# Half of wq of two heads, loaded onto partitions 0 to 63 by transfers that run on four DMA engines

## The chip, the cores and the metric

The kernel runs on one NeuronCore of a Trainium2 chip. The core has five instruction streams that run side by side and wait for one another by semaphores: TensorE (PE; its weight loads are listed as PEld), VectorE (DVE), ScalarE (ACT), GpSimd (POOL) and SyncE (SP), which here issues nearly all the transfers. Sixteen DMA engines move the data from HBM, the chip's main memory, into SBUF, the on-chip memory of 128 partitions; TensorE writes its products into PSUM. The metric is the device time of one launch in microseconds (us), lower is better.

## The reference

Two layers, each an attention block with a cached K and V and then a mixer block, are applied to two rows of 512 numbers:

```python
B, Sq, D = 2, 1, 512
Hq, Hkv, Sk, Dh = 32, 8, 32768, 128
x = x + _A_ref(_layernorm(x), A_k_cache, A_v_cache, A_wq, A_wo)   # attention
x = x + _B_ref(_layernorm(x), B_w1, B_b1, B_w2, B_b2)             # mixer
x = x + _A_ref(_layernorm(x), A_k_cache, A_v_cache, A_wq, A_wo)
x = x + _B_ref(_layernorm(x), B_w1, B_b1, B_w2, B_b2)
# _A_ref: q = x @ wq; scores = q k^T * Dh**-0.5; p = softmax(scores); o = p v; return o @ wo
# _B_ref: u = gelu(h * w1 + b1) over F = 1792; y = u @ w2 + b2
```

Each of the 2 x 8 pairs of a batch row and a KV head has 32768 keys and 32768 values of 128 float32 numbers, 16.8 MB of each. Both layers read the same caches and the same weights. The caches of all pairs do not fit in SBUF, so the second layer reads most of them again: the profile counts 1063 MB read from HBM. All arithmetic is float32.

## The kernel before

**Units.** The work of one (layer, batch row, head) is a unit. It has a K phase and a V phase of 64 column groups each, a group being 128 partitions x 512 numbers. A step is four groups of one phase. `Order` writes out the sequence of steps: the K phase of a unit alternates with the V phase of the unit before it. In K steps `k_step` (L360) multiplies four query rows with the keys into a PSUM tile `scores`; softmax parts run on VectorE and ScalarE; in V steps `v_step` (L428) multiplies the exponentials with the values into `acc`. At a unit's end `out_1` and `out_2` (L471, L492) multiply with wo into the PSUM tile `rows`. At the two places where a batch row passes from layer 0 to layer 1 the mixer runs between V steps, and the query of the next layer waits for it.

**Memory.** All keys, values and weights land in one SBUF tile `mem` of 106 cells, a cell being one group (2 KB per partition). A cell is free again when its last reader has run.

**Order of the loads.** `plan_loads` walks a list of what will be asked for, in the order of the steps, and gives each load a place in `mem` and a step behind which it may be issued; its own cost numbers choose between places. All loads are issued by SP, in that order, through one queue (q1 in the profile; the function `load`, L899 for weights, L904 for K and V). SP issues in program order: a load whose cells are not free yet holds up all the loads behind it. The usual load of keys or values is half a phase, 32 cells, 8 MB, and two to three such loads are under way or queued at a time, so that a load lands some 50 us after its issue.

**Weights.** wq and wo of a head are 128 partitions x 2048 numbers each, 1 MB, four cells. wq of the head is asked for 16 steps ahead of the first K step that uses it and is free again at that step. For heads 6 and 7 the weights stay for both layers; for the others they are loaded once in each layer. `wide_products` (L325) multiplies the layernormed input `xw` (four pieces of 128 partitions x 32 columns, one for each quarter `d` of the 512 inputs) with the quarter `d` of wq. The result is the raw query of the head in PSUM tile `bcast`, with one quarter's partial sum in each group of 32 partitions; `narrow_products` (L332) adds the quarters and puts them into `qz`, from which `k_step` reads.

**What other traffic there is.** ACT issues three small transfers on a queue of its own, q10: the input columns, the small weights `cols`, and one row of 512 results (2 KB, one partition) from `row` to `out_dram`. The last result leaves on SP's queue as four rows of 128. The page of the profile also lists two queues of kind "instruction", q8 and q14. They carry the program itself: q8 moved 1.23 MB, which for the 19128 matmuls and weight loads of the page is 64 bytes each.

Of the kernel before, what the change touches and what calls it, by code (L numbers as in the profile page):

```python
# [8 lines left out]
F32 = mybir.dt.float32  # L9
# [4 lines left out]
P = 128  # L14
# [24 lines left out]
STEP_US = 1.6  # L39
ASK_Q = 16  # L40
ASK_O = 8


class Order:
# [75 lines left out]
def plan_loads(order, weights, busy):  # L120
# [24 lines left out]
    while i < len(asked) or weights:  # L145
        if weights and (i == len(asked) or weights[0][0] <= asked[i][0]):
            _, name, last = weights.pop(0)
            label, sizes, stays = ("W", name, 0), (WCELLS,), True
        else:
            _, kind, u, g = asked[i]  # L150
            label, stays = (kind, u, g), (kind, u, g) in order.kept
            n = 1
            while (
                i + n < len(asked)
                and asked[i + n][1:] == (kind, u, g + n)
                and (g + n) % HALF
                and ((kind, u, g + n) in order.kept) == stays
            ):
# [44 lines left out]


@with_exitstack
def gqa_mixer_kernel(ctx: ExitStack, tc: tile.TileContext, x, kt, v, wqo, cols, out):
    nc = tc.nc
    B, D = out.shape
    HKV = wqo.shape[0]
# [43 lines left out]
    misc = pfix.tile([P, G], F32, name="misc")  # L253
    S = [const.tile([P, G], F32, name=f"S{k}") for k in range(2)]
    xw = const.tile([P, DT, 32], F32, name="xw")
    RAW = B
    xT = {}
    turn = [0, 0, 0]
# [23 lines left out]
    def first_input():  # L282
# [16 lines left out]
        for b in range(B):  # L299
            xT[b] = xcols[:, b, :]  # L300
            nc.vector.tensor_scalar_mul(xw[:, :, b], cen[:, b, :], rs[:, b : b + 1])

    def row_tile():
        return work.tile([P, D], F32, name="row", bufs=1)

# [15 lines left out]
    def wide_products(us, wq):  # L321

        q_ps[us] = pfix.tile([P, G], F32, name="bcast")
        for d in range(DT):
            nc.tensor.matmul(q_ps[us][32 * d : 32 * d + 32, :], xw[:, d, :], wq[:, d, :], start=True, stop=True)  # L325

    def narrow_products(us, side):

# [487 lines left out]
    for u in order.units:  # L816
# [60 lines left out]
        at(e + 3, unread, u, G)  # L877
        at(e + 4, change_3, y, us=1.0)
        at(e + 4, unread, u, G // 2)
        assert e + 4 < first["K", y]  # L880

    for x, _, y in order.changes:
# [10 lines left out]
    def load(label, n, a):  # L893
        kind, u, g = label
        if kind == "W":
            part, layer, h = u
            w = D * R
            at_w = 0 if part == "q" else w
            nc.sync.dma_start(cells(a, n), wqo[h][:, at_w : at_w + w])  # L899
            (wq_sb if part == "q" else wo_sb)[layer, h] = cells(a, n).rearrange("p (t c) -> p t c", t=DT)  # L900
            return
        layer, b, h = u
        src = (kt if kind == "K" else v)[b * HKV + h, g // HALF, :, (g % HALF) * G : (g % HALF + n) * G]
        nc.sync.dma_start(cells(a, n), src)  # L904
# [10 lines left out]
        load(label, n, a)  # L915
    constants()
    first_input()
    for step in range(3):
        make_q(opening_q, step)
    for p, (kind, u, g) in enumerate(steps):  # L920
# [8 lines left out]
def _layout(A_x, A_k_cache, A_v_cache, A_wq, A_wo, B_w1, B_b1, B_w2, B_b2):  # L929
# [9 lines left out]
    none = np.zeros_like(w2)  # L939
    w2z = np.stack([none, w2], axis=2).reshape(P, -1)  # L940
    cols = [w1, b1, w2z, none[:, :1], np.broadcast_to(B_b2.reshape(1, 1), (P, 1))]
    return {
        "x": np.ascontiguousarray(A_x.reshape(B * (D // P), P).T),
        "kt": np.ascontiguousarray(kt).reshape(U, 2, DH, HALF * G),
        "v": A_v_cache.reshape(U, 2, P, HALF * G),
        "wqo": np.concatenate([wq.reshape(HKV, P, -1), wo.reshape(HKV, DH, -1)], axis=2),
        "cols": np.concatenate(cols, axis=1),
    }


_INS = ["x", "kt", "v", "wqo", "cols"]


# [20 lines left out]
```

## Time and profile before

| what | value |
|---|---|
| time, median of 3 runs | 2498.51 us (2497.92 to 2499.63) |
| time of the profiled execution | 2500.69 us |
| its span, first to last instruction | 2498.9 us |
| read from HBM | 1063.29 MB, 426 GB/s over the span |
| busy: TensorE matmul / VectorE / ScalarE | 54% / 8% / 8% |
| DMA engines, mean busy share in each of the first 39 of 40 slices | 9 tenths or more |
| granted TensorE clock, mean | 0.765 |

The profiled execution is 2.2 us longer than the median of the runs. In the page, the digits of part 2 are tenths of busy time in 40 equal slices; part 4 follows the work that ended last back to its start; part 5 groups instructions by line. In an answer on DMA for a short stretch of time, "packets" counts the records that start in that stretch, "under 512 B" those of them that are smaller than 512 bytes. Among them is one record of 4 bytes for each DMA engine that has finished its part of a transfer: the engine's count on the semaphore of that transfer. A transfer on sixteen engines has sixteen such marks. The records do not say which engine they stand on.

### The profile page before, as it was taken

The numbers are of one execution on the slowest core, as the hardware profiler recorded it, in microseconds if no ns is written. First come the engines' busy times: TensorE is split into PE (matmuls) and PEld (weight loads), VectorE is DVE, ScalarE is ACT, GpSimd is POOL, SyncE is SP. The second block draws the span as 40 slices with busy tenths as digits, with TensorE's granted clock in tenths as the row PEclk, the third lists the DMA queues.
The fourth block names the chain that finished last, engine by engine and source line by source line (L and its number), as shares of the span: only waits on it lengthen the run. The fifth ranks groups of instructions, "written<-read, shape, count | busy, mean of one in ns | idle before, by whom it ended". The sixth has DMA issues, their size and how long they took to land.

```text
span 2498.9 us, 21072 instructions
## 1 busy us (share of the span) xinstructions
PE 1343.6 (54%) x9564; PEld 376.6 (15%) x9564; DVE 211.3 (8%) x600; ACT 187.4 (8%) x582; POOL 5.2 (0%) x18
## 2 busy tenths in 40 slices
PE   3445455545445544556775774555444544464567
PEld 1111111111111111111121221111111111111113
DVE  1000000000000000001110110000000000000012
ACT  0100000000000000001110210000000000000021
POOL 0000000000000000000000000000000000000000
PEclk8777777777777767778887886777777777777788
DMA  9999999999999999999999999999999999999996
GB/s 419 435 435 431 430 435 432 433 427 436 434 431 435 433 431 428 430 432 411 408 429 422 410 429 435 432 430 436 432 434 431 434 436 430 434 427 435 433 432 280
DMA packets 34946, 1064.64 MB, mean 426 GB/s; under 512 B 4133, under 2 KB 4137, under 8 KB 5034
## 3 DMA queue, kind: packets, MB, share of 16 engines
q1 hardware_dynamic: 34568, 1063.27, 99.1%
q8 instruction: 75, 1.23, 0.2%
q14 instruction: 13, 0.11, 0.0%
q10 hardware_dynamic: 290, 0.04, 0.0%
HBM read 1063.29 MB, written 0.00 MB: 426 GB/s over the span
## 4 chain that ended last, share of the span: by engine, by line
DMA 63%; PE 24%; another core or an unknown queue 11%; DVE 1%; issue 0%; ACT 0%; SPq 0%; POOLq 0%; POOL 0%; DVEq 0%; ACTq 0%
DMA mem<-in_v_dram 35%; DMA mem<-in_kt_dram 28%; PE acc L428 13%; PE scores L360 8%; PE misc L332 1%; PE rows L492 0%; PE bcast L325 0%; PE misc L384 0%; PE misc L451 0%; PE misc L657 0%; SPq L904 0%; ACT S L410 0%; PE misc L378 0%; PE misc L471 0%
## 5 line engine op out<-in xcount | busy, mean ns | idle before, releaser
L428 PE MATMUL acc<-mem,S 128*16 128x512 f32 x4080 | 598.9, 719 | 589.9 <-DMA mem<-in_v_dram 581.6
L360 PE MATMUL scores<-mem,qz 128*32 128x512 f32 x4096 | 598.6, 726 | 532.1 <-DMA mem<-in_kt_dram 532.1
L410 ACT ACTIVATE S<-S,neg 128x128 f32<-128x128 f32 x256 | 129.6, 509 | 2213.0 <-DVE S L405 1188.9
L360 PEld LDWEIGHTS scores<-mem,qz 128*32 128x32 f32 x4096 | 142.8, 127 | 915.0 <-issue 819.5
L428 PEld LDWEIGHTS acc<-mem,S 128*16 128x16 f32 x4080 | 127.5, 107 | 904.5 <-issue 818.8
L370 DVE TENSOR_REDUCE mx<-scores 128x1 f32<-128x512 f32 x64 | 44.3, 692 | 797.5 <-PE scores L360 789.7
L405 DVE STREAM_TRANSPOSE S<-scores 128x512 f32<-128x512 f32 x64 | 45.5, 711 | 125.1 <-PE acc L428 125.1
L410 ACT ACTIVATION_READ_ACCUMULATOR S<-S,neg 128x1 f32 x256 | 47.8, 187 | 0.0
L492 PE MATMUL rows<-mem,oz 128*2 128x512 f32 x248 | 44.1, 794 | 0.3 <-DVE oz L481 0.3
L380 DVE TENSOR_REDUCE m<-misc 1x4 f32<-1x128 f32 x32 | 8.9, 279 | 381.4 <-PE misc L378 381.4
L453 DVE RECIPROCAL rl<-misc 128x4 f32<-128x4 f32 x32 | 5.8, 183 | 382.1 <-PE misc L451 382.1
L462 DVE SCALAR_TENSOR_TENSOR row<-acc,quad,row 128x128 f32<-128x128 f32 x96 | 33.7, 351 | 3.4
L460 DVE TENSOR_SCALAR row<-acc,quad 128x128 f32<-128x128 f32 x32 | 11.2, 351 | 172.7 <-PE acc L428 172.7
L481 DVE TENSOR_TENSOR oz<-misc,rl 128x4 f32<-128x4 f32 x32 | 5.2, 162 | 222.8 <-PE misc L471 222.3
L471 PEld LDWEIGHTS misc<-head,row 128*128 128x128 f32 x64 | 14.0, 274 | 52.2 <-issue 38.3
L325 PE MATMUL bcast<-mem,xw 128*32 128x512 f32 x144 | 20.7, 636 | 1.7 <-POOL x_rs L298 1.7
L451 PEld LDWEIGHTS misc<-both,one 128*128 128x128 f32 x64 | 13.8, 271 | 49.7 <-issue 46.8
L471 PE MATMUL misc<-head,row 128*128 128x4 f32 x64 | 16.8, 334 | 7.3 <-DVE row L462 7.3
L332 PEld LDWEIGHTS misc<-selg,row 128*128 128x128 f32 x128 | 17.3, 210 | 19.6 <-issue 10.2
L576 ACT ACTIVATE row<-bcast,bias,scale 128x512 f32<-128x512 f32 x21 | 16.3, 778 | 38.1 <-PE rows L560 16.1
L332 PE MATMUL misc<-selg,row 128*128 128x2 f32 (+1 forms) x128 | 18.7, 268 | 0.8 <-DVE row L317 0.8
L378 PE MATMUL misc<-ident,mxa 128*1 128x128 f32 x64 | 17.0, 360 | 2.0 <-DVE mxa L376 2.0
(137 smaller groups left out, 282.1 us busy)
## 6 DMA issues: line engine op xcount, KB each, us to landing
mem<-in_v_dram SPq DMA_DIRECT2D x13, 4096.0 KB, 25.1
mem<-in_v_dram SPq DMA_DIRECT2D x37, 1024.0 KB, 9.5
mem<-in_kt_dram SPq DMA_DIRECT2D x15, 2048.0 KB, 18.1
mem<-in_kt_dram SPq DMA_DIRECT2D x30, 1024.0 KB, 9.9
mem<-in_wqo_dram SPq DMA_DIRECT2D x28, 1024.0 KB, 38.5
mem<-in_kt_dram SPq DMA_DIRECT2D x6, 4096.0 KB, 29.4
mem<-in_kt_dram SPq DMA_DIRECT2D x2, 6144.0 KB, 25.1
mem<-in_v_dram SPq DMA_DIRECT2D x3, 2048.0 KB, 38.3
```

Of the source, the lines that this page charges most:

```text
L325: nc.tensor.matmul(q_ps[us][32 * d : 32 * d + 32, :], xw[:, d, :], wq[:, d, :], start=True, stop=True)
L332: nc.tensor.matmul(pt[:, r * n : (r + 1) * n], q_row[us][:, r * DH : (r + 1) * DH], side, start=True, stop=True,)
L360: nc.tensor.matmul(sc_ps[u, half][32 * row : 32 * row + 32, :], qz[:, at : at + 32], cells(at_cell["K", u, g], 1), start=(i == 0), stop=(i ...
L370: nc.vector.tensor_reduce(mx[u][:, half : half + 1], sc_ps[u, half], axis=AX.X, op=ALU.max)
L378: nc.tensor.matmul(pm[:1, :P], mxa, ident, start=True, stop=True)
L405: nc.vector.transpose(S[half], sc_ps[u, half])
L410: nc.scalar.activation(s[:, :, h], s[:, :, h], AF.Exp, bias=neg[u][:, h : h + 1], scale=SCALE, accum_out=lsum[u][:, half, h : h + 1],)
L428: nc.tensor.matmul(acc[32 * row : 32 * row + R * QT, :], S[half][:, col : col + R * QT], vc, start=(g < NG), stop=(g >= quads - NG),)
L462: nc.vector.scalar_tensor_tensor(asb[u], acc[:, t * DH : (t + 1) * DH], quad[:, t : t + 1], asb[u], op0=ALU.mult, op1=ALU.add)
L471: nc.tensor.matmul(po_of[u][:, :R], asb[u], head, start=True, stop=(u != order.last))
L492: nc.tensor.matmul(rows[32 * r : 32 * r + B, :], oT[u][:, 2 * r + 1 - b : 2 * r + 3 - b], wo_of(u)[:, r, :], start=False, stop=(u == order ...
L576: nc.scalar.activation(hid[key, f], px[key], AF.Gelu_apprx_tanh, bias=shift[key][:, f : f + 1], scale=slope[key][:, f : f + 1],)
```

## The change

Two loads of wq are changed, `LOWER`: that of head 5 in layer 0 and that of head 1 in layer 1. The 26 other weight loads stay as they are. Of these two, the first half (quarters d = 0 and 1; 128 partitions x 1024 numbers, 512 KB) is loaded as before. The second half (quarters 2 and 3, also 512 KB) comes by two transfers of 256 KB from a new input array `low`. Each goes to 32 partitions x 2048 numbers: the first to partitions 0 to 31, the second to 32 to 63, in four cells of their own, so that the whole weight now takes six cells in place of four. On the side of HBM each of these transfers reads four groups of 8 rows, and a ninth row of zeros between the groups keeps them from being one run: the outermost size of the source is 4. A partition p of these 64 holds, for each of the two quarters, the 512 numbers of input row p and behind them those of input row 64 + p. `low` holds all eight heads, of which two are read.

`wide_products` then needs two matmuls of 64 rows in place of one of 128 for the quarters 2 and 3. The upper 64 partitions of `xw` for these quarters are copied onto partitions 0 to 63 of a new tile `high` by `lift`, once at the start and once behind each passage to layer 1. The scratch space for dynamic DMA is halved (256 to 128).

```diff
+LOWER = (("q", 0, 5), ("q", 1, 1))
+LOWER_CELLS = 6
...
-            label, sizes, stays = ("W", name, 0), (WCELLS,), True
+            label, sizes, stays = ("W", name, 0), (LOWER_CELLS if name in LOWER else WCELLS,), True
...
+    high = const.tile([P // 2, DT // 2, 32], F32, name="high")
...
+    def lift():
+
+        nc.vector.tensor_copy(high, xw[P // 2 :, DT // 2 :, :])
...
         for d in range(DT):
-            nc.tensor.matmul(q_ps[us][32 * d : 32 * d + 32, :], xw[:, d, :], wq[:, d, :], start=True, stop=True)
+            to = q_ps[us][32 * d : 32 * d + 32, :]
+            if d < DT // 2 or wq.shape[1] == DT:
+                nc.tensor.matmul(to, xw[:, d, :], wq[:, d, :], start=True, stop=True)
+                continue
+            half, k = P // 2, d - DT // 2
+            nc.tensor.matmul(to, xw[:half, d, :], wq[:half, DT // 2 + 2 * k, :], start=True, stop=False)
+            nc.tensor.matmul(to, high[:, k, :], wq[:half, DT // 2 + 2 * k + 1, :], start=False, stop=True)
...
+        at(e + 7, lift)
...
+            if u in LOWER:
+                nc.sync.dma_start(cells(a, DT // 2), wqo[h][:, : w // 2])
+                for k in range(2):
+                    to = cells(a + DT // 2, DT)[32 * k : 32 * k + 32, :]
+                    nc.sync.dma_start(to, low[h, k][:, :8, :])
+                wq_sb[layer, h] = cells(a, n).rearrange("p (t c) -> p t c", t=n)
+                return
...
+    low = np.zeros((HKV, 2, 4, 9, 4 * G), np.float32)
+    part = wq[:, :, D // P // 2 :, :].reshape(HKV, 2, 2, 4, 8, -1, G).transpose(0, 2, 3, 4, 5, 1, 6)
+    low[:, :, :, :8, :] = part.reshape(HKV, 2, 4, 8, 4 * G)
...
-    nc = bacc.Bacc("TRN2", target_bir_lowering=False, num_devices=1, dynamic_dma_scratch_size=256)
+    nc = bacc.Bacc("TRN2", target_bir_lowering=False, num_devices=1, dynamic_dma_scratch_size=128)
```

On SP, around the load of wq for head 5 in layer 0, the issues and their waits were these (the last number is partitions x numbers; `mem_74` is the SBUF tile `mem`, `in_wqo_dram` the weights; the names behind "waits" are semaphores, those of DMA lanes and that of TensorE, `PE_49`):

```order
L904 DMA mem_74<-in_kt_dram 128x16384 [waits DMAHW3_49,PE_49]
L899 DMA mem_74<-in_wqo_dram 128x2048 [waits DMAHW7_49]
L904 DMA mem_74<-in_v_dram 128x16384 [waits DMAHW4_49,PE_49]
L899 DMA mem_74<-in_wqo_dram 128x2048 [waits PE_49]
L904 DMA mem_74<-in_v_dram 128x16384 [waits DMAHW5_49,PE_49]
```

and are now these, with the new array as `in_low_dram`:

```order
L925 DMA mem_74<-in_kt_dram 128x16384 [waits DMAHW3_49,PE_49]
L914 DMA mem_74<-in_wqo_dram 128x1024 [waits DMAHW7_49]
L917 DMA mem_74<-in_low_dram 32x1x2048 [waits PE_49]
L917 DMA mem_74<-in_low_dram 32x1x2048
L925 DMA mem_74<-in_v_dram 128x16384 [waits DMAHW4_49]
L920 DMA mem_74<-in_wqo_dram 128x2048 [waits PE_49]
L925 DMA mem_74<-in_v_dram 128x16384 [waits DMAHW5_49,PE_49]
```

One issue became three, and the wait for TensorE that held the wo load now stands at the first of the two `in_low_dram` issues, ahead of the V load, which has to wait behind it. The loads ahead and behind keep their sequence, their sizes and, but for the wo load that follows (cells 6 to 9 in place of 4 to 7), their cells. The planner puts the changed load 11 steps later, behind step 274 in place of 263 (850 in place of 839 for the second one), since the two more cells were last read by wo of the unit before, and with it the V load behind it 3 steps later. At the second load, that of head 1 in layer 1, the same rows change in the same way.

On TensorE, in the V steps of the unit that runs when the changed wq has come, before:

```order
L428 MATMUL acc<-mem,S_91 16x512 x12
L325 MATMUL bcast<-mem,xw 32x512 x4
L428 MATMUL acc<-mem,S_91 16x512 x4
L428 MATMUL acc<-mem,S_92 16x512 x8
L451 MATMUL misc<-both,one 128x4
```

and now:

```order
L441 MATMUL acc<-mem,S_91 16x512 x12
L334 MATMUL bcast<-mem,xw 32x512 x2
L337 MATMUL bcast<-mem,xw 32x512
L338 MATMUL bcast<-mem,high 32x512
L337 MATMUL bcast<-mem,xw 32x512
L338 MATMUL bcast<-mem,high 32x512
L441 MATMUL acc<-mem,S_91 16x512 x4
L441 MATMUL acc<-mem,S_92 16x512 x8
L464 MATMUL misc<-both,one 128x4
```

Four matmuls became six, in the same place among the V matmuls.

More of the change, by code (lines that the diff above doesn't have):

```diff
@@ L205, in gqa_mixer_kernel @@
 @with_exitstack
-def gqa_mixer_kernel(ctx: ExitStack, tc: tile.TileContext, x, kt, v, wqo, cols, out):
+def gqa_mixer_kernel(ctx: ExitStack, tc: tile.TileContext, x, kt, v, wqo, low, cols, out):
     nc = tc.nc
@@ L917, in gqa_mixer_kernel @@
     first_input()
+    lift()
     for step in range(3):
@@ L946, in _layout @@
         "wqo": np.concatenate([wq.reshape(HKV, P, -1), wo.reshape(HKV, DH, -1)], axis=2),
+        "low": low,
         "cols": np.concatenate(cols, axis=1),
     }
-_INS = ["x", "kt", "v", "wqo", "cols"]
+_INS = ["x", "kt", "v", "wqo", "low", "cols"]
 def kernel(A_x, A_k_cache, A_v_cache, A_wq, A_wo, B_x, B_w1, B_b1, B_w2, B_b2):
```

## The prediction

> **What bounds the kernel now.** I read the page first.
>
> ```profile
> span 2498.9 us, 21072 instructions
> ...
> DMA  9999999999999999999999999999999999999996
> GB/s 419 435 435 431 430 435 432 433 427 436 434 431 435 433 431 428 430 432 411 408 429 422 410 429 435 432 430 436 432 434 431 434 436 430 434 427 435 433 432 280
> DMA packets 34946, 1064.64 MB, mean 426 GB/s; under 512 B 4133, under 2 KB 4137, under 8 KB 5034
> ...
> q8 instruction: 75, 1.23, 0.2%
> ...
> q10 hardware_dynamic: 290, 0.04, 0.0%
> ...
> DMA 63%; PE 24%; another core or an unknown queue 11%; DVE 1%; issue 0%; ACT 0%; SPq 0%; POOLq 0%; POOL 0%; DVEq 0%; ACTq 0%
> ```
>
> The DMA engines are busy in every slice but the last, at up to 436 GB/s, which is 27.2 GB/s for each of the sixteen. The chain that ended last is mostly transfers. The stages say the same: from 100 to 2470 us the DMA share is 1.00 or 1.01 (at 417 GB/s in the stage in the middle, where layer 0 passes to layer 1), and TensorE is busy half the time.
>
> ```profile
> core 0: us, PE busy (x) PEld busy (x) DVE busy (x) ACT busy (x) POOL busy (x), PEclk, DMA share, GB/s
> 100.00:1100.00 1000.00, 502.94 (x3510) 135.50 (x3510) 70.73 (x199) 52.84 (x200) 0.00 (x0) 0.74 1.00 432
> 1180.00:1450.00 270.00, 190.71 (x1368) 54.53 (x1372) 36.13 (x108) 44.36 (x104) 2.17 (x4) 0.83 1.01 417
> 1450.00:2470.00 1020.00, 541.82 (x3795) 150.46 (x3788) 79.23 (x219) 69.37 (x228) 0.54 (x1) 0.76 1.00 432
> ```
>
> So bytes bound the kernel, and the change moves no byte more or less. What it changes is which engines carry them. That matters only if the engines are not equally late, so I looked at the end marks (records of 4 bytes) of single 8 MB loads: early in the run; just ahead of the first changed load (five stretches: 702.0 to 702.45, to 703.8, 703.8 to 705.2, 705.2 to 707.7); just ahead of the second (2055.0 to 2055.7, to 2056.9, 2058.2 to 2060.4); near the end (2416.25 to 2416.535, to 2418.5, 2418.5 to 2420.9, 2420.9 to 2423).
>
> ```profile
> DMA packets 37, 1.38 MB, mean 510 GB/s; under 512 B 16, under 2 KB 16, under 8 KB 16
> ...
> DMA packets 9, 0.33 MB, mean 728 GB/s; under 512 B 4, under 2 KB 4, under 8 KB 4
> DMA packets 22, 0.92 MB, mean 510 GB/s; under 512 B 8, under 2 KB 8, under 8 KB 8
> DMA packets 7, 0.46 MB, mean 328 GB/s; under 512 B 0, under 2 KB 0, under 8 KB 0
> DMA packets 27, 1.25 MB, mean 498 GB/s; under 512 B 8, under 2 KB 8, under 8 KB 8
> ...
> DMA packets 10, 0.39 MB, mean 563 GB/s; under 512 B 4, under 2 KB 4, under 8 KB 4
> DMA packets 23, 0.98 MB, mean 517 GB/s; under 512 B 8, under 2 KB 8, under 8 KB 8
> DMA packets 19, 0.72 MB, mean 328 GB/s; under 512 B 8, under 2 KB 8, under 8 KB 8
> ...
> DMA packets 13, 0.40 MB, mean 1387 GB/s; under 512 B 6, under 2 KB 6, under 8 KB 7
> q10 hardware_dynamic: 2, 0.00, 2.0%
> DMA packets 25, 0.99 MB, mean 438 GB/s; under 512 B 9, under 2 KB 9, under 8 KB 10
> DMA packets 16, 1.05 MB, mean 437 GB/s; under 512 B 0, under 2 KB 0, under 8 KB 0
> DMA packets 23, 0.98 MB, mean 468 GB/s; under 512 B 8, under 2 KB 8, under 8 KB 8
> ```
>
> At 62.9 to 65.6 us all sixteen engines end a load within 2.7 us. At 702 eight end within 1.8 us, then none for 1.4 us, then the other eight; from the fourth to the last it is 707.7 - 702.45 = up to 5.2 us. At 2055 it is 2060.4 - 2055.7 = 4.7 us, at 2416 up to 6.4 us. Eight engines fall behind. All sixteen get the same bytes of data, so something else takes their time, and the only other traffic of any size is the program itself:
>
> ```profile
> q8 instruction: 19, 0.31, 0.2%
> ```
>
> This is the queue's row for 0 to 705 us: 19 fetches, over eight engines 2.4 each, for a lag of 3 to 5 us, so an estimated 1.5 us of an engine per fetch. A consumer waits for all sixteen marks. The lagging eight are the ones that set the end, and a byte taken from them should be time.
>
> **The change, part by part.** *The bytes.* An engine carries 1 MB / 16 = 64 KB of a weight. Now it carries 32 KB in the first half, and four engines carry 256 KB / 4 = 64 KB of each of two transfers on top: 160 KB for these four, 32 KB for the other twelve. At 27.2 GB/s the twelve save 1.2 us and the four lose 3.6 us. If the four are among the leading ones, they need a lead of 3.6 + 1.2 = 4.8 us over the last. They have 5.2 at the first load. They have 4.7 at the second, and the gap grows from there to 6.4. Then the load ends 1.2 us earlier on the engines that set its end: -1.2 us twice, **-2.4 us**.
>
> Do the four lead? The page's 4133 records under 512 B are 289 of q10's 290 and 3844 others, which is 240 x 16 + 4. SP issues 241 loads and stores, all of 128 rows but the last, of four rows: a transfer whose outermost size is four does run on four engines. [...] The row of q10 above is the store of one row of 512 results, one data record and one mark. It had to stand between two records of some engine, and its mark falls with the first five marks of the big load: the engine that takes a one-row transfer is one of the five earliest. [...]
>
> *The later issue.* SP now holds three loads back until wo of the unit before is used.
>
> ```profile
> 679.89 0.41 SPq L899 DMA_DIRECT2D mem<-in_wqo_dram  x1
> 699.12 0.33 SPq L904 DMA_DIRECT2D mem<-in_v_dram  x1
> 713.07 0.33 SPq L899 DMA_DIRECT2D mem<-in_wqo_dram  x1
> 718.22 0.33 SPq L904 DMA_DIRECT2D mem<-in_v_dram  x1
> ...
> 711.97 1.03 PE L492 MATMUL rows<-mem,oz 128*2 128x512 f32 x8
> 727.65 9.22 PE L360 MATMUL scores<-mem,qz 128*32 128x512 f32 x64 [9.50 <-DMA mem<-in_kt_dram]
> 749.49 3.39 PE L428 MATMUL acc<-mem,S 128*16 128x512 f32 x16 [12.61 <-DMA mem<-in_v_dram]
> 757.61 1.04 PE L325 MATMUL bcast<-mem,xw 128*32 128x512 f32 x8
> ```
>
> The first half still goes at about 680. The two others and the V load of 699 go at 713, when L492 has run, and then wo: four issues of some 0.4 us, until 715. The K load ahead lands at 727.6, and even the leading engines, 6 us ahead, have work until 721. No engine runs dry, so the 33 and 14 us of delay cost nothing; the cover is 6 us. The weight still lands in its turn, by 732, and is read at 757.6. What is queued behind the held issues on SP is only the load of 718. The second place has the same spacing.
>
> *TensorE* does two more matmuls per changed load (L325 took 1.04 us for four, so +0.5 us) in V steps ahead of which it stood idle for 12.61 us: nothing. *VectorE* copies 64 x 64 numbers three times:
>
> ```profile
> 15.24 0.23 DVE L346 COPY qz<-misc 128x4 f32<-128x4 f32 x2 [1.96 <-PE misc L332]
> 26.03 8.47 PE L360 MATMUL scores<-mem,qz 128*32 128x512 f32 x64 [10.82 <-DMA mem<-in_kt_dram]
> ```
>
> Small copies take 0.15 us there, and the opening has 10.82 us of cover ahead of the first keys. The scratch space is not on any path here.
>
> *The sum*: against the profiled execution, 2500.69 - 2.4 = 2498.3 us; the median of the runs stands 2.18 lower, 2498.51 - 2.4 = **2496.1 us**. This is 0.1%, half of the 0.2% that a measurement of this kernel can about tell from no change.
>
> **The rivals.** *The four are not all leaders (slower).* If one of them is among the lagging eight, it gets +3.6 us each time, and the end with it: +7.2, 2505.7 us. It decides from a single lagging engine on. [...]
>
> *The two narrow loads share a way into SBUF with other engines.* [...] 128 KB take 4.8 us alone and 9.6 us at half rate: the four would be 8.4 us later relative to their old place, against a lag of the others of 5.2 to 6.4 us that has grown by 1 us or so until a stage's end. That is +1 to +2 us instead of -1.2 each time, together about +3: 2501.6 us. I take nothing for the sum, as the rate per engine in all rows is that of one engine alone. [...]
>
> *It doesn't do what it says.* Between 1100 and 1450 the engines wait for one another anew (loads of 1 MB with waits on TensorE), and the 1.2 us of the first load could be lost there: 2497.3 us; with both lost, 2498.5 us. Against it: the DMA share of this stage is 1.01.
>
> **How the numbers follow.** The forecast has 0.60 (its own range, with the 0.9 us by which the runs shown scatter, is 2494.9 to 2497.5). Nothing or half of it has 0.12, sharing 0.14, lagging engines among the four 0.14. The range is 2494.5 to 2503.0: it leaves out the lagging case and a little at each end. Slower by over 0.2% (over 2503.5) is the lagging case and the worst of sharing, 0.18; faster by over 0.2% would need over twice the bytes' worth, 0.04; within it 0.78.
>
> **What would show it.** Right: in the changed kernel's marks at 720 to 732 us four engines that led end the narrow loads with or just ahead of the lagging eight, and from there on the gap of 1.4 us without marks at the 8 MB loads is filled; the K and V loads behind land 1.2 us earlier, and 2.4 us earlier after 2110. Wrong: a mark more than 5 us behind the lagging eight after a changed load (a lagging engine hit, or shared writes), or TensorE waiting at L325.

## The result and the profile after

The changed kernel takes 2507.03 us (median of 7 runs, 2506.23 to 2508.17), against 2498.16 us for the kernel before in the same comparison (7 runs, 2497.92 to 2499.63). The ratio is 1.0034, 95% interval 1.0023 to 1.0046: slower by 8.9 us. The forecast was 2496.1 us, with a range up to 2503.0.

The page of the changed kernel's profiled execution (2506.23 us), in the rows that were shown of before:

```profile
span 2504.4 us, 21095 instructions
...
DMA  9999999999999999999999999999999999999996
GB/s 419 434 434 433 430 433 429 435 430 435 430 400 436 433 432 434 423 434 415 418 430 423 417 426 435 433 433 434 429 432 430 437 433 401 430 433 434 433 429 288
DMA packets 35090, 1064.64 MB, mean 425 GB/s; under 512 B 4149, under 2 KB 4153, under 8 KB 5306
...
q8 instruction: 75, 1.23, 0.2%
...
DMA 68%; PE 22%; another core or an unknown queue 8%; ACT 1%; issue 0%; DVE 0%; SPq 0%; POOLq 0%; POOL 0%; ACTq 0%; DVEq 0%
```

Transfers make up 68% of the chain that ended last, against 63% before; among the runs below this share goes from 62% to 67% with no relation to the time, so it settles nothing. The bytes are the same, to the last digit shown. The DMA engines are as busy as before in every slice, yet two slices, the twelfth and the thirty-fourth, moved only 400 and 401 GB/s. A slice is 62.6 us, so they are the stretches from 689 to 751 and from 2066 to 2129 us: the two places of the change. A busy share of 9 tenths and more at 400 GB/s says that transfers got longer, not that engines waited.

What SP issued around the first place was as described and as expected (columns: start, duration, line, transfer):

```profile
678.85 0.41 SPq L914 DMA_DIRECT2D mem<-in_wqo_dram  x1
...
714.06 1.48 SPq L917 DMA_DIRECT2D mem<-in_low_dram  x2
715.59 0.44 SPq L925 DMA_DIRECT2D mem<-in_v_dram  x1
716.08 0.43 SPq L920 DMA_DIRECT2D mem<-in_wqo_dram  x1
```

TensorE's six matmuls, in the groups of the stretch from 740 to 775 us (two records each), took 1.0 + 1.1 + 1.0 = 3.1 us, where the four of before took 1.04: 2.1 us more, not the 0.5 that was said, and why is not shown. They held up nothing; the idle time was ahead of a V load, as before:

```profile
L441 PE MATMUL acc<-mem,S 128*16 128x512 f32 x64 | 9.5, 721 | 15.0 <-DMA mem<-in_v_dram 15.0
L337 PE MATMUL bcast<-mem,xw 64*32 64x512 f32 x4 | 1.1, 601 | 0.0
L338 PE MATMUL bcast<-mem,high 64*32 64x512 f32 x4 | 1.0, 589 | 0.0
L334 PE MATMUL bcast<-mem,xw 128*32 128x512 f32 x4 | 1.0, 592 | 0.0
```

For a comparison by stages I take a second, more usual execution of the kernel before (2498.98 us; the one behind the prediction was 2500.69). Its two stretches of 60 us around the places, with the DMA share and GB/s as the last two columns:

```profile
core 0: us, PE busy (x) PEld busy (x) DVE busy (x) ACT busy (x) POOL busy (x), PEclk, DMA share, GB/s
...
700.00:760.00 60.00, 30.37 (x214) 8.20 (x214) 2.60 (x7) 1.62 (x8) 0.00 (x0) 0.72 1.00 430
...
2050.00:2110.00 60.00, 29.02 (x218) 7.85 (x210) 4.17 (x11) 2.11 (x8) 0.00 (x0) 0.72 1.00 431
```

And those of the changed kernel:

```profile
700.00:760.00 60.00, 25.87 (x178) 7.12 (x182) 2.62 (x7) 2.12 (x8) 0.00 (x0) 0.72 1.00 401
...
2050.00:2110.00 60.00, 24.51 (x178) 6.23 (x174) 3.73 (x9) 2.11 (x8) 0.00 (x0) 0.71 1.00 400
```

At a DMA share of 1.00 in both, 29 of 430 and 31 of 431 GB/s are missing: 60 x 29 / 430 = 4.0 us and 60 x 31 / 431 = 4.3 us, 8.3 us together. It is a short stretch inside that does it. These are the rows of the changed kernel for 715 to 733.7 and for 735 to 740 us:

```profile
DMA packets 314, 6.42 MB, mean 343 GB/s; under 512 B 40, under 2 KB 40, under 8 KB 168
...
DMA packets 33, 2.11 MB, mean 423 GB/s; under 512 B 0, under 2 KB 0, under 8 KB 0
```

In the single records behind these rows the slow stretch is sharp. It lasts from 723.0 to 733.7 us, while the narrow transfers are under way: 10.6 us, where 128 KB per engine would take 4.8. In it 50 of the 64 records of 8 KB take 0.46 to 0.68 us (usual: 0.31) and a record of 64 KB up to 4.58 us (usual: 2.42). At 728 us sixteen records are in flight, one for each engine, and not one has its usual length: eight of 64 KB with 3.9 to 4.6 us, four of 8 KB with 0.54 to 0.65 us, four of 4 KB with 0.30 to 0.34 us (usual: 0.16). So it is not only the four engines of the narrow transfers that were slowed, but all sixteen.

### The profile page after: what moved, and what is told of

Read it like the earlier page. It is cut to its first block, busy times and chain, and to the rows that moved or that the text cites. A ratio compares the mean times of both kernels' runs of the same rounds, so it can differ in the third digit from the quotient of the medians.

```text
span 2504.4 us, 21095 instructions
## 1 busy us (share of the span) xinstructions
PE 1346.0 (54%) x9572; PEld 376.3 (15%) x9572; DVE 212.0 (8%) x603; ACT 187.8 (7%) x582; POOL 5.2 (0%) x18
## 2 busy tenths in 40 slices
DMA packets 35090, 1064.64 MB, mean 425 GB/s; under 512 B 4149, under 2 KB 4153, under 8 KB 5306
## 4 chain that ended last, share of the span: by engine, by line
DMA 68%; PE 22%; another core or an unknown queue 8%; ACT 1%; issue 0%; DVE 0%; SPq 0%; POOLq 0%; POOL 0%; ACTq 0%; DVEq 0%
DMA mem<-in_v_dram 35%; DMA mem<-in_kt_dram 33%; PE acc L441 12%; PE scores L373 7%; PE misc L345 0%; PE rows L505 0%; PE bcast L334 0%; PE misc L397 0%; PE misc L464 0%; SPq L925 0%; ACT S L423 0%; ACT mem L781 0%; PE misc L391 0%; PE misc L484 0%
```

## The theories

- **D, destination:** an engine that writes partitions which another engine is writing slows both, and with them the rest. It rests on an assumption of the author's about which partitions an engine writes in a load of 128 rows: these are called its own here, and the others foreign to it. No record names an engine or a partition, so no run shows the assumption. By it the four engines of the changed kernel write foreign partitions.
- **S, source or share:** reading grouped rows, or giving four engines so much at once, is what is slow.
- **L, laggards:** one of the four is a lagging engine (the prediction's first rival).
- **P, place:** the later issue, the six cells, the lift or the layout of memory cost the time.

How many engines carry a transfer is read from its end marks: the page of before counts 4133 records under 512 B and that of the changed kernel 4149, 16 more, as each of the two weights has 16 + 4 + 4 marks in place of 16. So each narrow transfer runs on four engines.

All kernels below differ from the changed kernel or from the one before by the edit shown, and were timed against the kernel before on the same chip; that stood at 2498.12, 2497.98, 2498.14, 2498.06 and 2498.16 us in the five comparisons.

## What made the two places slow

**The control: everything but the narrow transfers.** Six cells are kept free, the issue is late, lift and scratch are as changed, but the weight comes by one plain load.

```diff
-            if u in LOWER:
+            if False:
...
-            nc.sync.dma_start(cells(a, n), wqo[h][:, at_w : at_w + w])
+            nc.sync.dma_start(cells(a, 4), wqo[h][:, at_w : at_w + w])
```

> The two weights are loaded plainly (one transfer of 128 x 2048, sixteen engines) into four of the six cells, so that only the later issue, the lift copies and the cells are left of the change. If the narrow transfers themselves cost the 8.9 us, whatever the mechanism: 2498.2 us, within 1 us of the kernel before, and all 8 KB records of these loads near 0.31 us. If the later issue on SP or the two more cells cost it: 2503 to 2507 us.

Measured: 2500.34 us (11 runs, 2500.11 to 2502.3), ratio 1.0009 (1.0000 to 1.0018). The first place moved 434 GB/s and the second 430, with no slow record:

```profile
700.00:760.00 60.00, 31.12 (x210) 8.43 (x214) 2.84 (x8) 2.11 (x8) 0.00 (x0) 0.72 1.01 434
2050.00:2110.00 60.00, 28.68 (x202) 7.75 (x198) 4.17 (x11) 2.11 (x8) 0.00 (x0) 0.74 1.00 430
```

So 6.7 us of the loss come with the narrow transfers, and 2.2 us do not. These 2.2 us are taken up in the next section.

**The same bytes to the same 64 partitions, by all sixteen engines.** One transfer of 64 rows from a source without groups, on sixteen engines (4165 records under 512 B: 16 + 16 marks for a weight). By the assumption some of the engines then write foreign partitions.

```diff
-                for k in range(2):
-                    to = cells(a + DT // 2, DT)[32 * k : 32 * k + 32, :]
-                    nc.sync.dma_start(to, low[h, k][:, :8, :])
+                nc.sync.dma_start(cells(a + DT // 2, DT)[: P // 2, :], low[h])
```

> The second half goes to the same 64 partitions, but as one transfer of 64 rows on sixteen engines, four rows each. [...] Theory S (few engines, or the source in spaced groups, are what slows all): 2498.2 us, records at 0.31 and 2.42 us. Theory L (lagging engines among the four, no slowing of records): 2498.2 us.

Measured: 2509.69 us (5 runs, 2509.24 to 2511.59), ratio 1.0048 (1.0035 to 1.0061). The places are slower still than in the changed kernel:

```profile
700.00:760.00 60.00, 26.58 (x174) 7.10 (x174) 2.43 (x6) 2.11 (x8) 0.00 (x0) 0.69 1.00 399
2050.00:2110.00 60.00, 24.60 (x182) 6.38 (x174) 3.73 (x9) 2.11 (x8) 0.00 (x0) 0.71 0.99 392
```

Neither four engines nor a source in groups is needed for the slow stretch. By D the author's estimate was 2499 to 2503 us, some 7 us too low. The slow stretch speaks against S; the next two runs turn it round, with the grouped source and then the four engines but, by the assumption, without foreign partitions.

**Grouped source, on own rows by the assumption.** As the changed kernel, but with eight groups of four rows, so that eight engines carry each of the two transfers of 32 rows (4165 records under 512 B: 16 + 8 + 8 marks for a weight). That these rows are the eight engines' own is the assumption; no run shows it.

```diff
-                    nc.sync.dma_start(to, low[h, k][:, :8, :])
+                    nc.sync.dma_start(to, low[h, k][:, :4, :])
...
-    low = np.zeros((HKV, 2, 4, 9, 4 * G), np.float32)
+    low = np.zeros((HKV, 2, 8, 5, 4 * G), np.float32)
```

> [...] Theory D: no collision, 8 KB records at 0.31 us, 64 KB records at 2.42 us, time 2498.2 - 2.4 = 2495.8 us if the eight are the leading eight, about 2500.6 if they are the lagging ones. Theory S: the slow stretch stays, 2501 to 2507 us. Theory L: 2500 us or more without a slow stretch.

Measured: 2502.14 us (11 runs, 2501.6 to 2504.86), ratio 1.0017 (1.0009 to 1.0026). No record at the two places is slow, and both stretches moved 432 GB/s:

```profile
700.00:760.00 60.00, 29.05 (x204) 7.99 (x206) 2.37 (x7) 2.11 (x8) 0.00 (x0) 0.72 1.00 432
2050.00:2110.00 60.00, 27.10 (x196) 7.16 (x188) 4.00 (x10) 2.11 (x8) 0.00 (x0) 0.74 1.00 432
```

So a grouped source does not make the slow stretch. The 1.8 us above the control fit another thing, which no run tests by itself: these eight get 32 KB more each (1.2 us) at each place, and the end marks behind the first place show two engines further back than any in the control, at 7.3 and 7.7 us behind the first in place of 4.9. By that reading, not all of these eight lead.

**Four engines, on own rows by the assumption.** Only the first 256 KB of the second half are loaded, by two transfers of sixteen rows to partitions 0 to 15 and 32 to 47, on four engines (4149 records under 512 B: 16 + 4 + 4 marks for a weight). The other 256 KB are left out, and the products read cells that were not filled.

```diff
-                for k in range(2):
-                    to = cells(a + DT // 2, DT)[32 * k : 32 * k + 32, :]
-                    nc.sync.dma_start(to, low[h, k][:, :8, :])
+                for j in range(2):
+                    to = cells(a + DT // 2, DT)[32 * j : 32 * j + 16, :]
+                    nc.sync.dma_start(to, low[h, 0][:, 4 * j : 4 * j + 4, :])
```

> [...] Theory D: no slow stretch; the twelve other engines have 32 KB less per place, 2495.8 us. Theory S: slow stretch of half the length, 2498.2 + 4.5 - 2 = about 2500 to 2502 us. Theory L: 2498 to 2502 us with records at 0.31 us.

Measured: 2497.91 us (11 runs, 2497.33 to 2499.63 but for one of 3868.91, which was not profiled and is not explained), ratio 0.9999 (0.9990 to 1.0009). No record at the two places is slow, so four engines with the grouped source do not make the slow stretch either: S falls. The time is 2.4 us below the control, which is what the prediction gave for 32 KB less on the twelve other engines twice. Part of these bytes is not loaded at all, so this alone doesn't show that four engines can carry all of it. It does show that none of its four engines lags, as a lagging one would have been set back by its 32 KB more, 1.2 us at each place: L falls, if they are the four of the changed kernel, which no record names.

**Its partner: the same 256 KB and source, again on four engines (4141 records under 512 B: 16 + 4 marks for a weight), to partitions 0 to 31.**

```diff
-                for k in range(2):
-                    to = cells(a + DT // 2, DT)[32 * k : 32 * k + 32, :]
-                    nc.sync.dma_start(to, low[h, k][:, :8, :])
+                to = cells(a + DT // 2, DT)[:32, :]
+                nc.sync.dma_start(to, low[h, 0][:, :8, :])
```

> The first 256 KB of the second half, to partitions 0 to 31 by one transfer of four groups of eight rows, as in the changed kernel; the other 256 KB are left out. [...] If foreign rows are the cause (D): half as many bytes collide as in the changed kernel, so a stretch of about 5 us with slow records on all engines twice, +2 to +2.5 us each, together +4 to +5: 2502 to 2503 us, slow 8 KB records (over 0.45 us) at both places. If the number of bytes on four engines, or their source, was the cause (S), the time is that of own rows, 2497.9, and no record is slow.

Measured: 2501.69 us (11 runs, 2501.24 to 2502.95), ratio 1.0015 (1.0006 to 1.0023): 3.8 us above its partner, with 22 slow records of 8 KB at each place (0.59 us in the mean), where the changed kernel has 50. The stretches:

```profile
700.00:760.00 60.00, 31.23 (x202) 8.36 (x202) 3.00 (x8) 2.11 (x8) 0.00 (x0) 0.69 1.01 420
2050.00:2110.00 60.00, 28.56 (x194) 7.66 (x190) 4.17 (x11) 2.11 (x8) 0.00 (x0) 0.72 1.00 416
```

and those of the partner:

```profile
700.00:760.00 60.00, 32.17 (x214) 8.51 (x218) 3.32 (x9) 2.12 (x8) 0.00 (x0) 0.74 1.01 434
2050.00:2110.00 60.00, 30.79 (x206) 8.32 (x208) 2.98 (x8) 2.11 (x8) 0.00 (x0) 0.72 0.99 428
```

Half the bytes cost about half of what the changed kernel loses. Besides the destination, the number of transfers differs, one of 32 rows in place of two of sixteen, and with it the rows in a group, eight in place of four. But the run with eight groups had transfers of 32 rows and no slow record, and the run on sixteen engines had no groups and was slow. So it is the destination: which engines write which of the rows.

**The narrow transfers alone.** Is writing a foreign partition slow in itself, or only while other engines write too? In the kernel before, the two transfers of the change are put ahead of the first load, which goes to the same cells and so waits for them.

```diff
+    a0 = next(a for label, _, a in begin[-1] if label[0] == "W")
+    for k in range(2):
+        nc.sync.dma_start(cells(a0, DT)[32 * k : 32 * k + 32, :], low[5, k][:, :8, :])
     for label, n, a in begin.get(-1, ()):
         load(label, n, a)
```

> The kernel before with the two narrow transfers of the change (512 KB, each engine eight rows of 32, to partitions 0 to 63) put ahead of the first load, which goes to the same cells and so waits for them: the four engines write while no other engine does. If the slowing needs two engines that write the same rows at once (D): the 8 KB records stand at 0.31 us each and the two transfers take about 5 us plus the start. If writing rows outside an engine's own is slow in itself (D2): the records stand at 0.5 us or more, as in the changed kernel (0.52 to 0.68), and the two take 9 us or more. The time is some 7 to 12 us above before by the wait, which says nothing.

Measured: 2506.62 us (one run; the wait it adds tells nothing). The load of wq waits on SP until 9.88 us, and between 4.5 and 8.5 us q1 carries nothing but the narrow transfers:

```profile
0.74 1.49 SPq L916 DMA_DIRECT2D mem<-in_low_dram  x2
9.88 0.36 SPq L899 DMA_DIRECT2D mem<-in_wqo_dram  x1
```

```profile
DMA packets 90, 0.40 MB, mean 100 GB/s; under 512 B 42, under 2 KB 42, under 8 KB 42
...
q1 hardware_dynamic: 54, 0.39, 23.3%
```

Of the 64 records of 8 KB, 60 stand at 0.309 us, the usual length; the first of each engine, 1.4 to 2.4 us, is the start. So this destination is not slow in itself; it takes other loads in flight at the same time. **That much of D is shown**: the destination, and other engines writing meanwhile. Whether two engines must write the same partition at once is not shown, and that the partitions are foreign to the engines that write them stays the author's assumption. Why all sixteen engines slow down was not settled here.

## Where the other 2.4 us came from

**The later issue alone, and all but the later issue.** First the kernel before with six cells kept for the two weights, loaded plainly:

```diff
+LOWER = (("q", 0, 5), ("q", 1, 1))
+LOWER_CELLS = 6
...
-            label, sizes, stays = ("W", name, 0), (WCELLS,), True
+            label, sizes, stays = ("W", name, 0), (LOWER_CELLS if name in LOWER else WCELLS,), True
```

> The kernel before with six cells reserved for the two weights, loaded plainly into four of them: only the later issue (11 steps for the weight, 3 for the V load behind) is left of the change; no lift, no tile, scratch as before. If the later issue costs 2.2 us (P): 2500.3. If not: 2498.1, and the 2.2 us lie in the rest.

Then the control with four cells, so that every issue stands where it stood before:

```diff
-LOWER_CELLS = 6
+LOWER_CELLS = 4
```

> The control of plain loads (2500.34 us) with the weight in four cells again: the plan and all issues are those of before. What remains of the change is the lift on VectorE, the tile for it, the scratch space and the unused input. If the later issue behind six cells costs the 2.2 us of the control (P), this one is at 2498.1, within 0.5 us of before. If the lift and the layout of memory cost them, it is at 2500.3.

And the kernel before once more, for its trace:

> The kernel before once more, for the trace of a usual execution: the profiled execution on which the prediction rests was 2500.69 us, 2.6 us above the median of all runs so far. Expected is 2497.9 to 2498.5. If the 2.2 us of the control are lost at the two places, its stages run level with the control's until 700 us and the control falls behind by about 1 us at each place; if they are lost at the start or the end, the difference stands there.

Measured: 2498.40 us (11 runs, 2497.73 to 2499.22; ratio 1.0001, 0.9992 to 1.0010) with the later issue alone, 2500.41 us (11 runs, 2500.13 to 2501.84; 1.0008, 0.9999 to 1.0017) with all but it, 2498.98 us for the kernel before (one run). The later issue costs nothing that can be measured, as the prediction had it. The trace of the control is not late at the two places; it falls behind little by little: the last end mark of a load comes 0.6 us later than in the run with the later issue at 610 us, 0.6 us at 1023 us, 1.0 us at 1196 us and 2.6 us near the end.

**Scratch space, input and lift one by one.** The kernel before with the smaller scratch space:

```diff
-    nc = bacc.Bacc("TRN2", target_bir_lowering=False, num_devices=1, dynamic_dma_scratch_size=256)
+    nc = bacc.Bacc("TRN2", target_bir_lowering=False, num_devices=1, dynamic_dma_scratch_size=128)
```

> The kernel before with the scratch space for dynamic DMA at 128 in place of 256, nothing else. The control with the plan of before stood at 2500.41 us, 2.4 above before, and the later issue alone at 2498.40: so the 2.4 us lie in the scratch space, the unused input, or the lift with its tile. If the scratch space is what costs (addresses in SBUF, or descriptors): 2500.4; if not, 2498.1.

with the unused input:

```diff
-_INS = ["x", "kt", "v", "wqo", "cols"]
+_INS = ["x", "kt", "v", "wqo", "low", "cols"]
```

> The kernel before with the array low (4.7 MB, of zeros) as one more input that nothing reads. If it is the unused input that costs, by moving the other arrays in HBM or by what is done ahead of the program: 2500.4; if not, 2498.1.

and the control of four cells without the input:

```diff
-_INS = ["x", "kt", "v", "wqo", "low", "cols"]
+_INS = ["x", "kt", "v", "wqo", "cols"]
```

> The control with the plan of before, but without the input low: scratch at 128, the tile high and the three copies on VectorE stay. If the lift costs the 2.4 us: 2500.4, and the runs with the scratch space or the input alone stand at 2498.1. If the input costs them: 2498.1. If the scratch space does, this one and the one with scratch alone are both at 2500.4.

Measured: scratch alone 2500.56 us (11 runs, 2500.16 to 2500.91; ratio 1.0009, 1.0001 to 1.0018), input alone 2498.28 us (11 runs, 2498.04 to 2500.07; 1.0002, 0.9993 to 1.0010), scratch and lift 2500.57 us (11 runs, 2500.03 to 2501.25; 1.0009, 1.0000 to 1.0018). Halving the scratch space, with no instruction added or moved, costs the whole 2.4 us. The lift costs nothing that can be measured.

**The space or the place?** The scratch space lies ahead of `mem` in each partition; in the built programs `mem` begins at byte 416 before and at byte 288 with the smaller scratch. Two runs keep scratch at 128 and put an unused tile ahead of `mem`, 32 numbers wide for byte 416 and 56 for byte 512:

```diff
+    pad = const.tile([P, 32], F32, name="pad")
     mem = const.tile([P, CELLS * G], F32, name="mem")
```

> Scratch at 128 as in the run that stood at 2500.56 us, with an unused tile of 128 bytes per partition ahead of mem, so that mem begins at byte 416 of each partition again, as before, in place of 288. If the place of mem is what cost 2.4 us: 2498.1. If the size of the scratch space itself did: 2500.5.

> The same with 224 bytes, so that mem begins at byte 512, a round address. If the place matters, this says in which sense: by the number of 512-byte pieces that a row of 2 KB or more touches, a round start should be no worse than 416 (2498.1) and perhaps faster by about 2 us more (2496); if only the distance from 416 matters, it is slower. If the size of the scratch space matters: 2500.5.

The third gets to byte 256 without a pad, by declaring `xcols` behind `mem`:

```diff
-    xcols = const.tile([P, B, DT], F32, name="xcols")
-    nc.scalar.dma_start(xcols, x)
     mem = const.tile([P, CELLS * G], F32, name="mem")
+    xcols = const.tile([P, B, DT], F32, name="xcols")
+    nc.scalar.dma_start(xcols, x)
```

> Scratch at 128 and the tile xcols declared behind mem instead of ahead of it: mem begins at byte 256 of each partition, and no space is spent on a pad. So far: 288 gave 2500.56 us, 416 gave 2498.04, 512 gave 2489.79. If a start at a multiple of 256 is enough: 2489.8. If it takes 512: the first piece of a row up to the next 512 is 256 bytes at 256, 224 at 288, 96 at 416, and by those the time should be near 2500.

Measured, with the length of all transfer records added up and divided by sixteen engines:

| `mem` begins at | time, median (runs) | ratio to before | records per engine | mean 64 KB record |
|---|---|---|---|---|
| 288 (scratch 128) | 2500.56 us (11) | 1.0009, 1.0001 to 1.0018 | 2482.4 us | 2425.4 ns |
| 416 (scratch 128 and pad) | 2498.04 us (11) | 1.0001, 0.9992 to 1.0010 | 2480.2 us | 2424.3 ns |
| 512 (scratch 128 and pad) | 2489.79 us (6) | 0.9970, 0.9958 to 0.9981 | 2472.5 us | 2420.8 ns |
| 256 (`xcols` behind) | 2490.01 us (5) | 0.9968, 0.9956 to 0.9981 | 2472.1 us | 2420.5 ns |

The place decides, not the space, and it does so by the length of the records: what an engine's records add up to moves with the time. Records are shorter at 256 and 512: in the median 309 ns for one of 8 KB, in place of 312 (416) and 313 (288), and in the mean 3.5 to 4.9 ns less for one of 64 KB. A record of 8 KB loses about as much as one eight times as long, so the cost goes by the record, one for each row of a load, and not by its bytes. The bytes moved between 100 and 1100 us show it too, first with `mem` at 288, then before (416), then at 512:

```profile
DMA packets 10067, 431.65 MB, mean 432 GB/s; under 512 B 1120, under 2 KB 1120, under 8 KB 1376
```

```profile
DMA packets 10069, 431.78 MB, mean 432 GB/s; under 512 B 1120, under 2 KB 1120, under 8 KB 1376
```

```profile
DMA packets 10085, 432.78 MB, mean 433 GB/s; under 512 B 1120, under 2 KB 1120, under 8 KB 1376
```

1.00 MB more in the same 1000 us is 2.3 us of transfers, over the whole run most of the 8 us. The kernels at 256 and 512 compute everything, and are 8 us faster than the kernel before and 17 us faster than the changed one.

256 does as well as 512, and 288 and 416 do worse. So it is not the number of 512-byte pieces that a row touches: for a row of 8 KB that is 17 at 256, 288 and 416 alike, and 16 at 512. Of the two slow starts 288 is the slower, 2425.4 against 2424.3 ns. What makes a record longer at these two is not shown. Both are odd multiples of 32, so these four runs do not tell whether a multiple of 64 or 128 would be enough.

## Both causes taken away

**The changed kernel with `mem` at byte 256.** The edit to the changed kernel is that of the last diff.

> The changed kernel as it is, with mem at byte 256. If the address and the foreign rows are independent: the kernel with mem at 256 alone, plus two slow stretches, minus the shift, that is plus 6.5 us (2507.03 - 2500.56). If the slow stretches come from rows that begin off a boundary (D3), they go with it and the time is 2.4 us below the kernel with mem at 256 alone.

Measured: 2496.00 us (11 runs, 2495.29 to 2497.82), ratio 0.9991 (0.9983 to 1.0000), so 6.0 us above the plain kernel at 256, near the 6.5 that were expected if the two causes are independent. The slow stretches are still there, so they don't hang on the place of `mem`:

```profile
700.00:760.00 60.00, 28.71 (x198) 7.89 (x200) 2.14 (x6) 0.56 (x3) 0.00 (x0) 0.69 1.00 402
2050.00:2110.00 60.00, 30.35 (x204) 8.19 (x206) 2.14 (x6) 0.00 (x0) 0.00 (x0) 0.69 0.99 400
```

**All bytes of the change on four engines, on own rows by the assumption, with `mem` at byte 256.** All 512 KB are loaded, by four transfers of sixteen rows in place of two of 32, into eight cells in place of four, so ten in all. The products were not fitted to the new places of the numbers: they read the cells that the changed kernel reads, so this run is for the time of the transfers alone.

```diff
-LOWER_CELLS = 6
+LOWER_CELLS = 10
...
-                    to = cells(a + DT // 2, DT)[32 * k : 32 * k + 32, :]
-                    nc.sync.dma_start(to, low[h, k][:, :8, :])
+                    for j in range(2):
+                        to = cells(a + DT // 2 + DT * k, DT)[32 * j : 32 * j + 16, :]
+                        nc.sync.dma_start(to, low[h, k][:, 4 * j : 4 * j + 4, :])
```

> [...] If the shift is worth what the prediction said, 2.4 us, and the foreign rows were all that stood against it: 2.4 us less than the kernel with mem at 256 alone, and no record slow at the two places. If four engines cannot carry 128 KB more each (their lead too small), or the ten cells cost time: the same as that kernel or more.

Measured: 2487.88 us (5 runs, 2487.43 to 2490.5), ratio 0.9960 (0.9947 to 0.9974), which is 2.1 us below the plain kernel at 256 (5 runs, 2489.41 to 2491.39). One of these five runs lies among those of the plain kernel, so by these runs alone the gain is likely and not certain, and some thirty other loads lie in other cells. No record at the two places is slow:

```profile
700.00:760.00 60.00, 32.78 (x218) 8.66 (x218) 2.14 (x6) 0.24 (x2) 0.00 (x0) 0.72 1.00 431
2050.00:2110.00 60.00, 33.62 (x218) 8.77 (x218) 3.50 (x9) 2.11 (x8) 0.00 (x0) 0.73 1.00 431
```

The end marks of a load late in the run, in us behind the first mark, show how many engines were moved (before with its load that begins to end at 2276.8, the changed kernel at 2284.0, plain at 256 at 2268.8, this kernel at 2245.7):

```
before         0.0 0.02 0.14 0.18 0.24 0.84 1.38 2.14 | 4.65 4.75 4.95 5.04 5.4  5.59 5.88 5.89
changed        0.0 0.43 0.91 1.13 | 3.97 4.67 4.73 4.87 4.91 4.95 5.12 5.29 5.82 5.92 6.42 7.61
plain at 256   0.0 0.09 0.43 0.45 0.85 0.91 0.95 2.07 | 3.95 4.11 4.15 4.19 4.21 4.38 4.81 4.91
own, at 256    0.0 0.18 0.32 0.8  | 3.26 3.43 4.09 4.44 4.75 4.76 4.86 5.02 5.09 5.12 5.89 6.35
```

Before, eight lead and eight follow. With the change, four lead and twelve follow: the four that carry the narrow loads have fallen back among the laggards.

How far back is in the marks of this last run. At the first place the last lagging engine ended its half of wq at 726.86 us, and the four ended their last narrow load at 726.65, 727.15, 727.25 and 727.99 us; at the second place it was 2071.86 against 2070.98, 2071.33, 2072.13 and 2072.29 us. So three of the four, and then two, came out behind the engine that had been last, by up to 1.1 us. From the last mark of the K load ahead to that of the V load behind, this run gained 0.2 us on the plain kernel at 256 at the first place (725.65 to 747.30 against 725.00 to 746.81) and 0.8 at the second (2070.66 to 2091.64 against 2070.08 to 2091.81), not 1.2 each. Where the rest of the 2.1 us was gained is not shown.

A version of this that computes the products as well was not tried: its input columns would need a tile of 1 KB per partition.

**The sum.** The place of `mem` costs 2.4 us (2500.56 - 2498.14). The slow stretches cost 8.1 us (2496.00 - 2487.88), or 8.3 by the missing bytes of the windows. The shift brings 2.1 us. 2.4 + 8.1 - 2.1 = 8.4 of the measured 8.9 us; the rest is within the scatter of the runs. The last two terms both rest on the run with ten cells.

## The prediction, step by step

- *"Eight engines fall behind", and a byte taken from them is time:* right as far as it was tried. That the four engines lead was the author's estimate, as no run of before shows which engines carry a transfer of four groups; the end marks late in the run bear it out, with eight leaders before and four with the change. With all bytes by transfers of sixteen rows the forecast gain of 2.4 us came out as 2.1 us (2490.01 to 2487.88).
- *The lead* ("They have 5.2 at the first load"): read too favourably. It was counted from the fourth mark on, as if the four were the foremost. In the run on own rows with `mem` at 256 their narrow loads ended 6.15 to 6.19 us behind the marks at 720.50, 721.00, 721.06 and 721.81 us of the K load ahead, whose last mark is at 725.65 (matched by this equal distance, as the marks name no engine): leads of 5.2, 4.7, 4.6 and 3.8 us, three of them short of the 4.8 that were asked for. The sign of being right did not come either: "the gap of 1.4 us without marks" was not filled (742.58 to 744.07 us at the next 8 MB load, still 1.5 us), as the four went from the leading group straight into the lagging one.
- *Where the lag comes from* (fetches of the program, an estimated 1.5 us of an engine each): no run took it away, so it stays argued.
- *Of the later issue, "the 33 and 14 us of delay cost nothing":* right, 2498.40 against 2497.98 us.
- *TensorE and the lift, nothing:* right, 2500.57 us with the lift and 2500.56 without it; the matmuls took 2.1 us more in place of the 0.5 that was said, beside 15.0 us of idle time.
- *"The scratch space is not on any path here":* wrong by 2.4 us. No path of instructions leads through it; but it sets the address at which 1063 MB land, and this kernel is bound by just these loads.
- *"I take nothing for the sum", of sharing:* the step that failed. The row behind it, "the rate per engine in all rows is that of one engine alone", could not bear it: all loads that SP issued before have 128 rows, and none has the shape of the narrow ones. The rival put the cost on the right transfers, but not its size: that sharing would halve the rate of the four, from 4.8 to 9.6 us, was the author's estimate, which no run shows, and it came to +3 us in all, when the runs show all sixteen slowed for 10.6 us (the slow 8 KB records at 0.59 us in the mean, some at 0.68, more than double), 4 us lost at each place. It counted the four alone, and the cost fell on the other twelve too.
- *The rival of lagging engines among the four* (2505.7 us, the nearest of the numbers): wrong in its cause, as none of the four lags. By the time alone it would have seemed confirmed; that it came within 1.3 us of the measured 2507.03 is luck.
- The mark that would show it wrong, "more than 5 us behind the lagging eight", did not come either: since all sixteen were slowed, no engine fell far behind the others, and the loss stood in the bandwidth row instead.
- Two of its figures are off without bearing on this: +3 us on 2498.51 is 2501.5 and not 2501.6, and 0.9 us on either side of 2496.1 is 2495.2 to 2497.0, not 2494.9 to 2497.5.

## What to carry to other kernels

When the DMA engines are the bound, look at where a transfer writes before counting what each engine carries: here two transfers of 32 rows on four engines, to partitions 0 to 63, slowed every engine (401 and 400 GB/s in the two stretches, in place of 430 and 431), and the same bytes by four transfers of sixteen rows did not (431 in both). Look at the address too: moving the start of the large tile from byte 416 to 256 or 512 was worth 8 us of 2498 here, four times what the whole shift of bytes could bring, and a tile declared behind it in place of ahead did it. An edit that only makes room can move such an address, so compare the addresses of the large tiles before and after.

## What was not expected

- 512 KB written to partitions 0 to 63, on four engines or on sixteen, while other loads were under way, slowed all sixteen engines: from 0.31 us to as much as 0.68 us for a record of 8 KB, and from 2.42 to as much as 4.58 us for one of 64 KB (5.08 us when sixteen engines shared the narrow load), and back at once when it was over. Alone, the same transfers ran at the usual rate, 0.309 us for 60 of the 64 records of 8 KB.
- The start of the destination tile alone changed the time of a kernel with the same instructions from 2489.8 (byte 512) to 2498.0 (416) and 2500.6 us (288).
- The DMA share is 1.00 with the loss and without it. The loss is seen in the bytes moved per stretch (401 against 430 GB/s) and in the length of single records.
